# Expert pieces on pairs of token tiles with bf16 turns, and the pieces beside the score units gathered in a new order

## The chip, the cores and the metric

The kernel runs on one core of one Trainium2 chip. Times are device microseconds (us) of that core, over many executions. For one core an execution more than 1.5% above the fastest of the same kernel counts as slow. The limit for "faster" or "slower" is 2%.

Engines: PE is the matrix engine, PEld its weight loads, DVE the vector engine, ACT the scalar (activation) engine, POOL GpSimd, SP the engine that issues most DMA transfers. PSUM is the memory in which the tiles that PE writes are kept here (the kernel's pools psc and psm among them). The granted clock is the share of its full speed that the chip allowed PE, as the profile records it.

## The reference

```python
# clustered attention: a query sees only keys of its own cluster
q_assign = argmax(q_n @ c_n.T); k_assign = argmax(k_n @ c_n.T)      # 16 clusters per head
mask = q_assign[:, :, :, None] == k_assign[:, :, None, :]
scores = where(mask, q @ k.T / 8, -1e9)                              # B 4, H 8, S 768, D 64
x = (softmax(scores) @ v) laid out as [3072 tokens, 512]
# mixture of adapters: two of eight experts of rank 16 for each token
w = softmax of the two largest of x @ w_gate
out = x + sum over both of w * ((x @ A[e]) @ B[e])
```

## The kernel before

Work goes by pairs of heads, 16 of them, and a pair has three steps of 256 queries. In each step PE makes six score units (sc, two matmuls each; ACT takes the exponential into ET; DVE and POOL add up ET for the softmax sums, sp and sm) and twelve value products (od, seen as 24 matmuls in the trace). Four pairs make one batch, 768 tokens; the experts of a batch run during the next four pairs. The small pieces go into the gaps between the score units: each step has slots 0 to 5 (behind score unit 0 to 5), "pre" (ahead of the value products) and "post" (behind them).

The small pieces, by the name of the tile that PE writes: tp (turns of q and k), rt (cluster scores) and its turn rn, from which DVE makes mx and the one-hot rows oh; oT (oh turned), copied to os_ and sent by DMA into the score operands augA and augB; dp (softmax sums over partitions) and its turn dn; xp (turn of the output, scaled into xn); lp and lt (gate logits). "Turn" means a transpose on PE. All of them share three PSUM buffers.

```python
def prep_onehot(p):                       # rn: needs rs, the DVE copy of rt
    rn_ps = psm.tile([128, HS], F32, name="rn_ps", tag="m")
    for i in range(3):
        nc.tensor.transpose(rn_ps[:, i * 128:(i + 1) * 128], s["rs"][:, i * 128:(i + 1) * 128], ident_f[:])
    ...                                   # mx, then oh, on DVE
def moe_x(b, ts, t):                      # one token tile, four fp32 turns
    xx = psm.tile([128, NDC, 128], F32, name="xx", tag="m")
    for dc in range(NDC):
        nc.tensor.transpose(xx[:, dc, :], xn_of[b][:, t, dc * 128:(dc + 1) * 128], ident_f[:])
    xTb = mo.tile([128, NDC, 128], BF16, name="xTb")
    nc.scalar.copy(xTb[:], xx[:])
# moe_z: four matmuls, DVE copy z_s; moe_g: the gate, twelve small operations, mostly DVE;
# moe_t: zg on DVE, turn zT_ps, DVE copy zT
def moe_l(b, ts, t):
    dl = psm.tile([128, DX], F32, name="dl", tag="m")
    nc.tensor.matmul(dl[:], ms.pop((b, "t", t))[:], b_b[:])
    ot = mo.tile([128, DX], F32, name="ot", bufs=4)
    nc.vector.tensor_tensor(ot[:], dl[:], xn_of[b][:, t, :], ALU.add)
    nc.sync.dma_start(out_b[:, t, :], ot[:])          # 256 KB
...
        for n in range(NS - 1):
            for i in range(6):
                scores(*divmod(n + 1, NT), i)
                run(n, i)                 # the pieces of slot i
            run(n, "pre")
            for kc in range(T):
                pv(n // NT, n % NT * T + kc)
            run(n, "post")
        p = NP - 1                        # the end
        den_sum(p)
        while mq:                         # expert pieces that are left
            moe()
        den_turn(p)
        normalize(p, 0)
        normalize(p, 1)
        logit_tiles(p, [0, 1, 2, 3])
        queue_moe(B - 1, [0, 1, 2, 3])
        moe(3)
        for kc in range(T):
            pv(p, 2 * T + kc)             # the last value products
        moe(3)
        normalize(p, 2)
        logit_tiles(p, [4, 5])
        queue_moe(B - 1, [4, 5])
        while mq:
            moe()
```

The softmax here doesn't subtract the row's maximum and nothing guards it: scores larger than these inputs give would overflow.

## Time and profile before

377.38 us, median of 6 executions (376.52 to 379.69). The profiled one spans 377.7 us. The page's busy times, and the chain of waits that ended last, followed back from the last instruction, with shares of the span:

```profile
PE 346.8 (92%) x2866; PEld 242.1 (64%) x2872; DVE 275.9 (73%) x479; ACT 243.6 (65%) x449; POOL 187.4 (50%) x157
...
PE 75%; DVE 12%; DMA 5%; ACT 3%; issue 3%; SPq 1%; DVEq 0%; ACTq 0%
```

PE is nearly always busy and makes up three quarters of the chain, so a shorter PE stream should shorten the kernel. The PE timeline of a step shows how its score units are broken up. Columns: start, length, engine, line, operation, tiles, shapes, count, and in brackets an idle stretch with what ended it:

```profile
89.29 0.50 PE L244 MATMUL sc<-augA 80*128 80x256 f32 x2
89.63 0.40 PE L244 MATMUL sc<-augB 80*128 80x256 f32 x2
89.86 0.49 PE L295 MATMUL dn<-ident_f,ds 128*128 128x128 f32 x3
90.11 0.48 PE L244 MATMUL sc<-augA 80*128 80x256 f32 x2
90.50 0.55 PE L203 MATMUL rn_ps<-ident_f,rs 128*128 128x128 f32 x3
90.81 0.48 PE L244 MATMUL sc<-augB 80*128 80x256 f32 x2
91.13 0.38 PE L308 MATMUL xp<-ident_f,OT 128*128 128x128 f32 x2
...
101.87 0.47 PE L244 MATMUL sc<-augA 80*128 80x256 f32 x2 [0.48 <-ACT OT L274]
```

Lengths overlap (89.29 + 0.50 reaches past 89.63), so the distance from start to start is what a group costs. A unit that follows a unit takes about 0.235 us (89.63 to 89.86), one that follows another piece about 0.32 (90.81 to 91.13). The 0.48 us at 101.87 is laid to ACT's OT, which had been done for long; the program's own waits at that instruction include the DMA that brings the one-hot rows. Three stretches will be compared below. They are cut at the start of the third step's value products of pair 4 and of pair 14 (pairs are counted from 0): 124.87 us to the first cut, 212.87 us for pairs 5 to 14, and 39.97 us for the rest, "the end". Plain pairs, without expert work, repeat every 19.5 us, the others take 20.2 to 22.5.

### The profile page before, as it was taken

How to read it: one execution, taken by the hardware profiler on the slowest of the kernel's cores; microseconds unless marked ns; L12 is line 12 of the kernel's file. 1: busy time of each engine (PE TensorE's matmuls, PEld its weight loads, DVE VectorE, ACT ScalarE, POOL GpSimd, SP SyncE). 2: the span in 40 equal slices, each digit the busy share in tenths (PEclk: the TensorE clock that was granted, in tenths of full speed). 3: DMA queues.
4: the chain of work that ended last, by engine and by line, in shares of the span. 5: the costliest groups of instructions: out<-in, count | busy, mean ns of one | idle time of the engine just before them, and what ended most of it. 6: DMA issues, size and time to landing. Idle time of an engine off the chain costs nothing.

```text
span 377.7 us, 7587 instructions
## 1 busy us (share of the span) xinstructions
PE 346.8 (92%) x2866; PEld 242.1 (64%) x2872; DVE 275.9 (73%) x479; ACT 243.6 (65%) x449; POOL 187.4 (50%) x157
## 2 busy tenths in 40 slices
PE   8798699999999999999999999999999999999773
PEld 3475567676767766675767766675666777667441
DVE  3463275969689876788699875789689876788765
ACT  3374557677686877675686876675686877666321
POOL 1057154756556455457356455547457455556300
PEclk9959699999999999999999999999999999999998
DMA  9367652616171706146281705137271302020204
GB/s 168 69 166 149 137 126 44 146 32 160 22 168 21 169 12 130 50 103 170 78 196 22 169 8 128 55 90 183 76 197 25 83 7 45 14 77 28 86 9 159
DMA packets 66340, 35.66 MB, mean 94 GB/s; under 512 B 56960, under 2 KB 61056, under 8 KB 66304
## 3 DMA queue, kind: packets, MB, share of 16 engines
q1 hardware_dynamic: 64592, 34.76, 38.7%
q10 hardware_dynamic: 1712, 0.43, 0.6%
q8 instruction: 22, 0.36, 0.4%
q14 instruction: 14, 0.11, 0.1%
HBM read 19.45 MB, written 6.29 MB: 68 GB/s over the span
## 4 chain that ended last, share of the span: by engine, by line
PE 75%; DVE 12%; DMA 5%; ACT 3%; issue 3%; SPq 1%; DVEq 0%; ACTq 0%
PE od L269 30%; PE sc L244 18%; PE tp L172 4%; PE dp L282 3%; PE rt L191 3%; DVE sp L248 3%; PE lp L323 2%; PE xx L370 2%; PE warm_ps L100 2%; PE oT L220 2%; PE rn_ps L203 2%; ACT ET L245 2%; PE xp L308 2%; PE dn L295 2%; DMA augB<-augA 2%
## 5 line engine op out<-in xcount | busy, mean ns | idle before, releaser
L245 ACT ACTIVATE ET<-sc,expbias 128x512 f32<-128x512 f32 x288 | 180.3, 698 | 19.2 <-PE sc L244 17.8
L248 POOL TENSOR_TENSOR sp<-ET 128x512 f32<-128x512 f32 x48 | 71.3, 1486 | 153.9 <-ACT ET L245 153.9
L269 PE MATMUL od<-ET,v_nat 128*64 128x256 f32 x1152 | 137.3, 388 | 1.4 <-DVE zT L430 1.2
L269 PEld LDWEIGHTS od<-ET,v_nat 128*64 128x64 f32 x1152 | 79.5, 139 | 48.4 <-issue 11.5
L250 POOL TENSOR_TENSOR sp<-sp,ET 128x512 f32<-128x512 f32 x48 | 74.8, 1559 | 7.1 <-ACT ET L245 4.3
L244 PE MATMUL sc<-augA 80*128 80x256 f32 x288 | 70.5, 327 | 8.1 <-DMA augA<-os__424 3.4
L244 PE MATMUL sc<-augB 80*128 80x256 f32 x288 | 69.9, 325 | 0.2 <-DMA augB<-os__249 0.2
L244 PEld LDWEIGHTS sc<-augA 80*128 80x128 f32 x288 | 45.6, 196 | 31.7 <-issue 24.3
L274 ACT COPY OT<-od 128x256 f32<-128x256 f32 x48 | 17.8, 371 | 72.7 <-PE od L269 72.7
L250 DVE TENSOR_TENSOR sp<-sp,ET 128x512 f32<-128x512 f32 x48 | 59.3, 1235 | 3.8 <-ACT ET L245 3.0
L248 DVE TENSOR_TENSOR sp<-ET 128x512 f32<-128x512 f32 x48 | 33.4, 697 | 35.5 <-ACT ET L245 35.5
L251 DVE TENSOR_TENSOR sm<-sp 128x256 f32<-128x256 f32 x48 | 58.1, 1211 | 0.8
L244 PEld LDWEIGHTS sc<-augB 80*128 80x128 f32 x288 | 45.5, 197 | 2.8 <-ACT ET L245 0.8
L251 POOL TENSOR_TENSOR sm<-sp 128x256 f32<-128x256 f32 x48 | 38.2, 796 | 3.6
L312 DVE TENSOR_TENSOR xn<-xp,rr 128x256 f32<-128x256 f32 x48 | 19.9, 416 | 3.0 <-PE xp L308 2.8
L437 DVE TENSOR_TENSOR ot<-dl,xn 128x512 f32<-128x512 f32 x24 | 16.2, 682 | 7.2 <-PE dl L435 7.2
L308 PE MATMUL xp<-ident_f,OT 128*128 128x128 f32 x96 | 18.2, 272 | 0.0
L172 PE MATMUL tp<-ident_f,q_nat 128*128 128x128 f32 x96 | 16.0, 277 | 1.7 <-DMA q_nat<-in_q_dram 1.5
L374 ACT CAST xTb<-xx 128x512 bf16<-128x512 f32 x24 | 14.2, 599 | 5.0 <-PE xx L370 4.9
L172 PE MATMUL tp<-ident_f,k_nat 128*128 128x128 f32 x96 | 16.3, 282 | 0.0
L282 PE MATMUL dp<-sm,ones_138 128*32 128x384 f32 x128 | 14.2, 498 | 1.0 <-DVE sm L251 1.0
L340 DVE TENSOR_TENSOR lgp<-lt,rr 128x96 f32<-128x96 f32 x15 | 3.9, 258 | 15.1 <-PE lt L336 15.1
(187 smaller groups left out, 347.5 us busy)
## 6 DMA issues: line engine op xcount, KB each, us to landing
q_nat<-in_q_dram SPq DMA_DIRECT2D x32, 192.0 KB, 3.7
augB<-augA SPq DMA_DIRECT2D x16, 384.0 KB, 4.6
v_nat<-in_v_dram SPq DMA_DIRECT2D x16, 384.0 KB, 4.3
out_dram<-ot SPq DMA_DIRECT2D x24, 256.0 KB, 2.3
k_nat<-in_k_dram SPq DMA_DIRECT2D x30, 192.0 KB, 4.1
k_nat<-in_k_dram ACTq DMA_DIRECT2D x2, 192.0 KB, 4.7
b_f<-in_moe_B_dram SPq DMA_DIRECT2D x1, 256.0 KB, 4.4
a_f<-in_moe_A_dram SPq DMA_DIRECT2D x4, 64.0 KB, 3.0
```

The lines of the kernel that those rows point to most:

```text
L172: nc.tensor.transpose(tp[:, i * 128:(i + 1) * 128], src[:, t, :, :].rearrange("p a d -> p (a d)"), ident_f[:],)
L244: nc.tensor.matmul(sc[:, i, :], au[0:80, k0:k0 + 128], au[0:80, cs])
L245: nc.scalar.activation(ET[:, 2 * kp:2 * kp + 2, :], sc[:], ACTF.Exp, bias=expbias[:], scale=SCALE)
L248: eng.tensor_tensor(sp[:], ET[:, 0:2, :], ET[:, 2:4, :], ALU.add)
L250: eng.tensor_tensor(sp[:], sp[:], ET[:, 4:6, :], ALU.add)
L251: eng.tensor_tensor(s["sm"][a][:, cs], sp[:, 0, :], sp[:, 1, :], ALU.add)
L269: nc.tensor.matmul(s["od"][64 * a:64 * a + 64], s["v"][:, a, kc, :], s["ET", th][a][:, kc, :], start=(kc == 0), stop=(kc == T - 1), tile_p ...
L274: nc.scalar.copy(s["OT"][:, cs], s["od"])
L282: nc.tensor.matmul(dp[r:r + 32, :].rearrange("p (n i) -> p n i", i=128), ones32[:], s["sm"][a][:].rearrange("p (n h i) -> p h n i", h=2, i ...
L308: nc.tensor.transpose(xp[:, i, :, :].rearrange("p a d -> p (a d)"), s["OT"][:, t * 128:(t + 1) * 128], ident_f[:],)
L312: nc.vector.tensor_tensor(xn_of[b][:, ts, j * 128:(j + 1) * 128].rearrange("p t (a d) -> p t a d", a=2), xp[:], s["rr"][:, ts].to_broadcas ...
L437: nc.vector.tensor_tensor(ot[:], dl[:], xn_of[b][:, t, :], ALU.add)
```

## The change

Its intent: fewer, longer groups on PE (a unit behind a switch costs 0.32 us, not 0.235), with the one-hot pieces early enough to hide their DMA, and expert turns in bf16 on two token tiles at a time, so that half as many pieces and copies are needed. The core of the diff:

```diff
+PLAN = (   # piece, (step of the pair, slot); 6 is "pre", 7 is "post"
+    ("moe", (0, 1)), ("load_v", (0, 1)), ("t0", (1, 3)), ("moe", (1, 5)), ("moe", (1, 7)), ("t1", (2, 1)),
+    ("t2", (2, 1)), ("route", (2, 7)), ("load_qk", (2, 7)), ("den_sum", (2, 7)), ("onehot", (3, 1)),
+    ("den_turn", (3, 1)), ("norm0", (3, 4)), ("norm1", (3, 4)), ("mask", (3, 5)), ("logit_sum", (3, 7)),
+    ("logit_turn", (4, 3)), ("norm2", (4, 3)), ("queue", (4, 7)),
+)
-                put(n + 1, 4, prep_transpose, p + 2, 0)
-                put(n + 2, 0, prep_transpose, p + 2, 1)
-                put(n + 2, 2, prep_transpose, p + 2, 2)
-                put(n + 3, 2, prep_onehot, p + 2)
-                put(n + 4, 2, prep_mask, p + 2)
-                put(n + 3, 1, den_turn, p)
 ... (the other pieces likewise)
-            for i in ((0,), (3, 5), (3,))[n % NT]:
-                put(n, i, moe)
-    def moe_x(b, ts, t):
-        xx = psm.tile([128, NDC, 128], F32, name="xx", tag="m")
-            nc.tensor.transpose(xx[:, dc, :], xn_of[b][:, t, dc * 128:(dc + 1) * 128], ident_f[:])
+    def moe_x(b, ts, i):
+        xb = mo.tile([128, 2, DX], BF16, name="xb")
+        nc.vector.tensor_copy(xb[:], xn_of[b][:, t:t + 2, :])
+        xx = psm.tile([128, 2, NDC, 128], BF16, name="xx", tag="m")
+        for u in range(2):
+            for dc in range(NDC):
+                nc.tensor.transpose(xx[:, u, dc, :], xb[:, u, dc * 128:(dc + 1) * 128], ident_b[:])
 ... (moe_z, moe_t, moe_l likewise on two tiles; one store of 512 KB for two of 256 KB)
-        n = len(ts)
+        n = len(ts) // 2
```

More of the change, by code (lines that the diff above doesn't have):

```diff
@@ L69, with after @@
     st = {}
+    done = set()
+    def after(step, *needs):
+        assert all(x in done for x in needs), (step, needs)
+        done.add(step)
     def load_pair(p, which="qkv", keng=nc.sync):
@@ L163, in prep_transpose @@
     def prep_transpose(p, u):
+        after(("t", p, u), *[("t", p, i) for i in range(u)])
         s = st[p]
@@ L183, in prep_route @@
     def prep_route(p):
+        after(("route", p), ("t", p, 2))
         s = st[p]
@@ L199, in prep_onehot @@
     def prep_onehot(p):
+        after(("onehot", p), ("route", p))
         s = st[p]
@@ L216, in prep_mask @@
     def prep_mask(p):
+        after(("mask", p), ("onehot", p))
         s = st[p]
@@ L230, in scores @@
     def scores(p, th, ui):
+        after(("s", p, th, ui), ("mask", p))
         s = st[p]
@@ L274, in pv @@
             nc.scalar.copy(s["OT"][:, cs], s["od"])
+            after(("pv", p, th))
     def den_sum(p):
+        after(("den_sum", p), ("s", p, NT - 1, 5))
         s = st[p]
@@ L291, in den_turn @@
     def den_turn(p):
+        after(("den_turn", p), ("den_sum", p))
         s = st[p]
@@ L302, in normalize @@
     def normalize(p, th):
+        after(("norm", p, th), ("den_turn", p), ("pv", p, th))
         s = st[p]
@@ L317, in logit_sum @@
     def logit_sum(p):
+        after(("logit_sum", p), ("pv", p, NT - 1))
         s = st[p]
@@ L331, in logit_turn @@
     def logit_turn(p):
+        after(("logit_turn", p), ("logit_sum", p), ("den_turn", p))
         s = st[p]
@@ L365, with moe_z @@
     ms = {}
-    def moe_x(b, ts, t):
-        xx = psm.tile([128, NDC, 128], F32, name="xx", tag="m")
-        for dc in range(NDC):
-            nc.tensor.transpose(
-                xx[:, dc, :], xn_of[b][:, t, dc * 128:(dc + 1) * 128], ident_f[:],
-            )
-        xTb = mo.tile([128, NDC, 128], BF16, name="xTb")
+    def moe_x(b, ts, i):
+        t = ts[i]
+        xb = mo.tile([128, 2, DX], BF16, name="xb")
[4 more added lines that the diff above has]
+                nc.tensor.transpose(xx[:, u, dc, :], xb[:, u, dc * 128:(dc + 1) * 128], ident_b[:])
+        xTb = mo.tile([128, 2, NDC, 128], BF16, name="xTb")
         nc.scalar.copy(xTb[:], xx[:])
         ms[(b, t)] = xTb
-    def moe_z(b, ts, t):
+    def moe_z(b, ts, i):
         key = (b, "z", ts[0])
-        if t == ts[0]:
+        t = ts[i]
+        if i == 0:
             ms[key] = mo.tile([128, T, E * R], F32, name="z_s", bufs=1)
-        z = psm.tile([128, E * R], F32, name="z", tag="m")
+        z = psm.tile([128, 2, E * R], F32, name="z", tag="m")
         xTb = ms.pop((b, t))
-        for dc in range(NDC):
-            nc.tensor.matmul(z[:], xTb[:, dc, :], a_b[:, dc, :], start=(dc == 0), stop=(dc == NDC - 1))
-        nc.vector.tensor_copy(ms[key][:, t - ts[0], :], z[:])
+        for u in range(2):
+            for dc in range(NDC):
+                nc.tensor.matmul(z[:, u, :], xTb[:, u, dc, :], a_b[:, dc, :], start=(dc == 0), stop=(dc == NDC - 1))
+        nc.vector.tensor_copy(ms[key][:, i:i + 2, :], z[:])
     def moe_g(b, ts):
@@ L418, in moe_g, with moe_t, moe_l @@
         ms[(b, "g", ts[0])] = g
-    def moe_t(b, ts, t):
-        i = t - ts[0]
-        zg = mo.tile([128, E, R], BF16, name="zg")
+    def moe_t(b, ts, i):
+        zg = mo.tile([128, 2, E, R], BF16, name="zg")
         nc.vector.tensor_tensor(
-            zg[:], ms[(b, "z", ts[0])][:, i, :].rearrange("p (e r) -> p e r", e=E),
-            ms[(b, "g", ts[0])][:, i, :].unsqueeze(2).to_broadcast([128, E, R]), ALU.mult,
-        )
-        zT_ps = psm.tile([128, 128], BF16, name="zT_ps", tag="m")
-        nc.tensor.transpose(zT_ps[:], zg[:].rearrange("p e r -> p (e r)"), ident_b[:])
-        zT = mo.tile([128, 128], BF16, name="zT")
+            zg[:].rearrange("p u e r -> p (u e) r"),
+            ms[(b, "z", ts[0])][:, i:i + 2, :].rearrange("p u (e r) -> p (u e) r", e=E),
+            ms[(b, "g", ts[0])][:, i:i + 2, :].rearrange("p u e -> p (u e)").unsqueeze(2).to_broadcast([128, 2 * E, R]),
+            ALU.mult,
+        )
+        zT_ps = psm.tile([128, 2, 128], BF16, name="zT_ps", tag="m")
+        for u in range(2):
+            nc.tensor.transpose(zT_ps[:, u, :], zg[:, u].rearrange("p e r -> p (e r)"), ident_b[:])
+        zT = mo.tile([128, 2, 128], BF16, name="zT")
         nc.vector.tensor_copy(zT[:], zT_ps[:])
-        ms[(b, "t", t)] = zT
-    def moe_l(b, ts, t):
-        dl = psm.tile([128, DX], F32, name="dl", tag="m")
-        nc.tensor.matmul(dl[:], ms.pop((b, "t", t))[:], b_b[:])
-        ot = mo.tile([128, DX], F32, name="ot", bufs=4)
-        nc.vector.tensor_tensor(ot[:], dl[:], xn_of[b][:, t, :], ALU.add)
+        ms[(b, "t", ts[i])] = zT
+    def moe_l(b, ts, i):
+        zT = ms.pop((b, "t", ts[i]))
+        ot = mo.tile([128, 2, DX], F32, name="ot")
+        for u in range(2):
+            dl = psm.tile([128, DX], F32, name="dl", tag="m")
+            nc.tensor.matmul(dl[:], zT[:, u, :], b_b[:])
+            nc.vector.tensor_tensor(ot[:, u, :], dl[:], xn_of[b][:, ts[i] + u, :], ALU.add)
         out_b = out[b * S:(b + 1) * S, :].rearrange("(p t) d -> p t d", t=T)
-        nc.sync.dma_start(out_b[:, t, :], ot[:])
+        nc.sync.dma_start(out_b[:, ts[i]:ts[i] + 2, :], ot[:])
     mq = []
@@ L450, in queue_moe @@
     def queue_moe(b, ts):
-        n = len(ts)
+        if len(ts) == T:
+            for p in range(b * HP, (b + 1) * HP):
+                after(("moe", p), ("logit_turn", p), *[("norm", p, th) for th in range(NT)])
+        n = len(ts) // 2
         mq.append([("g", b, ts)])
@@ L454, in queue_moe @@
             for i in range(n + 1):
-                piece = [(first, b, ts, ts[i])] if i < n else []
+                piece = [(first, b, ts, 2 * i)] if i < n else []
                 if i > 0:
-                    piece.append((second, b, ts, ts[i - 1]))
+                    piece.append((second, b, ts, 2 * (i - 1)))
                 mq.append(piece)
@@ L481 @@
     with tc.manual_schedule(engines={PE}):
-        plans = [{} for _ in range(NP * NT + 4)]
+        plans = [{} for _ in range(NP * NT + 8)]
         def put(n, i, *call):
@@ L487 @@
         for p in range(NP):
-            n = NT * p
-            if p + 2 < NP:
-                put(n, 1, load_pair, p + 2, "v")
-                put(n + 1, 4, prep_transpose, p + 2, 0)
-                put(n + 2, 0, prep_transpose, p + 2, 1)
-                put(n + 2, 2, prep_transpose, p + 2, 2)
-                put(n + 3, 2, prep_onehot, p + 2)
-                put(n + 4, 2, prep_mask, p + 2)
-            if p < NP - 1:
-                put(n + 2, "post", den_sum, p)
-                if p + 2 < NP:
-                    put(n + 2, "post", prep_route, p + 2)
-                    put(n + 2, "post", load_pair, p + 3, "qk")
-                put(n + 3, 1, den_turn, p)
-                put(n + 3, 3, normalize, p, 0)
-                put(n + 3, 4, normalize, p, 1)
-                put(n + 3, "pre", logit_sum, p)
-                put(n + 4, 0, logit_turn, p)
-                put(n + 4, 1, normalize, p, 2)
-                if p % HP == HP - 1:
-                    put(n + 4, 1, queue_moe, p // HP, list(range(T)))
+            calls = {"load_v": (load_pair, p + 2, "v"), "load_qk": (load_pair, p + 3, "qk"),
+                     "t0": (prep_transpose, p + 2, 0), "t1": (prep_transpose, p + 2, 1),
+                     "t2": (prep_transpose, p + 2, 2), "route": (prep_route, p + 2),
+                     "onehot": (prep_onehot, p + 2), "mask": (prep_mask, p + 2),
+                     "den_sum": (den_sum, p), "den_turn": (den_turn, p),
+                     "norm0": (normalize, p, 0), "norm1": (normalize, p, 1), "norm2": (normalize, p, 2),
+                     "logit_sum": (logit_sum, p), "logit_turn": (logit_turn, p),
+                     "queue": (queue_moe, p // HP, list(range(T)))}
+            for name, (step, slot) in PLAN:
+                if name in ("den_sum", "den_turn", "norm0", "norm1", "norm2", "logit_sum", "logit_turn"):
+                    ok = p < NP - 1
+                elif name == "queue":
+                    ok = p < NP - 1 and p % HP == HP - 1
+                elif name == "load_qk":
+                    ok = p + 3 < NP
+                elif name == "moe":
+                    ok = True
+                else:
+                    ok = p + 2 < NP
+                if ok:
+                    put(NT * p + step, slot, *calls.get(name, (moe,)))
         put(0, 1, prep_onehot, 1)
@@ L511 @@
         NS = NP * NT
-        for n in range(NS):
-            for i in ((0,), (3, 5), (3,))[n % NT]:
-                put(n, i, moe)
         def run(n, i):
@@ L523 @@
                 run(n, i)
-            run(n, "pre")
+            run(n, 6)
             for kc in range(T):
                 pv(n // NT, n % NT * T + kc)
-            run(n, "post")
+            run(n, 7)
         p = NP - 1
```

## The prediction

> **What bounds it now.** PE is 92% busy (busy table) and holds 75% of the chain of waits; DVE holds 12%. After the prologue (about 45 us) each pair of heads is three steps: score units and small pieces, then a 2.74 us value product (od), and once per pair dp and rt, 1.43 us. Starts in the PE timeline: plain pairs repeat every 19.5 us (65.6, 85.1, 104.6); pairs with expert work take 20.2 to 22.5, about 7 us more per batch of four. Idle PE gaps (groups, waits) are small: 0.5 us per plain pair where the first score unit waits for the one-hot rows' DMA into augA (shown as waiting for ACT OT), and 0.65 to 0.75 us per expert pair where lp waits for DVE's oh. ACT (65%) and DVE (73%) are busy but looser.
>
> **What a group switch costs.** From start-to-start times on PE: a score unit after another takes 0.235 us, one after a different piece 0.32. A pair has 18.
>
> **What the change removes.**
> 1. Fewer groups: the plain pair goes from about 13 broken runs of units to 7. Sum over a pair: about 5.9 to 5.1 us.
> 2. The mask pieces come a whole step earlier, so the 0.5 us DMA wait goes.
> 3. Expert turns: six groups of four fp32 transposes (0.44 us each) per batch become three of eight bf16 ones (estimate 0.5 to 0.55 each, from oT at 75 ns and z at 50 to 60 ns per matmul): 1 us per batch. [...] Half as many expert pieces and fewer waits for zT: 0.7 us per batch.
>
> **What it adds.** Twelve casts of 128x1024 to bf16 on DVE. [...] the augA cast shows it (1536 columns in 0.953 us against 512 columns of sp in 0.697). Estimate 0.65 us each; most are hoisted into slack. Pairing z, zg, zT copies returns about half of that.
>
> **What gives part back.** The one-hot turns (rn) now come two units after dp, but need rs, which waits on DVE behind the previous step's sp and sm (1.3 + 1.3 us), which wait for the fifth exponential on ACT. Worked through with trace durations, rs lands about 2.8 us after od ends, while PE reaches rn at 2.0: a new wait of 0.7 to 1.0 us per pair. The second xp waits about 0.2 us for oh. So the plain pair comes to about 18.8 to 19.0 us, not the 17.9 of PE work alone: the loop exponential, sums, rs, rn, oh is nearly as long as PE's.
>
> **Sum.** 15 pairs x 0.6 = 9 us; experts 4 x 1.7 = 6 us less about 1 us at the end (one 512 KB store last instead of 256 KB). Predicted 364.0 us, range 354 to 373. Faster by over 2%: 0.74; within 2%: 0.24; slower: 0.02.
>
> **What would show it.** Right: plain pairs at 18.5 to 19.1 us; no score unit waiting for augA's one-hot DMA; score units mostly 0.235; rn waiting for DVE rs 0.5 us or more; xx groups at 0.5 to 0.6 us; DVE busy a few us higher; xb about 0.65 us. Wrong: rn not waiting and plain pairs at 18 us (then 355 or less).
>
> **What would make it wrong.** Bursts of four units with four PSUM buffers could stall on ACT; in expert steps DVE has 7 us in line before rs, so rn could wait 2 us; xb at 1 us or more if POOL contends; or rs comes earlier than reckoned, and the full gain appears.

What the profile of the kernel before shows is times alone: a load of 128x128 bf16 weights (z) took 98 ns, one of fp32 weights (tp, xp, xx) 140 to 145; the augA cast took 0.953 us for 1536 columns, which by proportion is 0.64 us for 1024, about the 0.65 estimated for a cast xb. The sum: as written it comes to 9 + 6 - 1 = 14 us (4 x 1.7 is 6.8, written as 6).

## The result

375.98 us median (372.07 to 380.46, 20 executions) against 378.05 for the kernel before in the same rounds (40 executions). The ratio of fast runs is 0.9901, 95% interval 0.9872 to 0.9931: a gain of 1%. A ratio here is the mean time of one kernel's fast runs over that of the other's of the same rounds, so it is not quite the ratio of the medians quoted. The prediction was 364.0 with a range of 354 to 373: wrong. The profiled run was 374.2 us long. Its busy times and chain:

```profile
PE 341.3 (91%) x2870; PEld 242.9 (65%) x2872; DVE 281.6 (75%) x455; ACT 243.2 (65%) x437; POOL 181.8 (49%) x157
...
PE 53%; DVE 25%; ACT 9%; issue 4%; DMA 4%; POOL 1%; SPq 1%; DVEq 0%; ACTq 0%; POOLq 0%
```

PE lost only 5.5 us of busy time, and its share of the chain fell from 75% to 53%: DVE and ACT have come into the chain. The same part of a plain pair as shown of before:

```profile
104.15 0.50 PE L260 MATMUL sc<-augA 80*128 80x256 f32 x2
104.49 0.39 PE L260 MATMUL sc<-augB 80*128 80x256 f32 x2
105.48 0.55 PE L217 MATMUL rn_ps<-ident_f,rs 128*128 128x128 f32 x3 [0.60 <-DVE rs L209]
105.86 0.49 PE L314 MATMUL dn<-ident_f,ds 128*128 128x128 f32 x3
106.11 0.48 PE L260 MATMUL sc<-augA 80*128 80x256 f32 x2
106.43 0.40 PE L260 MATMUL sc<-augB 80*128 80x256 f32 x2
106.67 0.40 PE L260 MATMUL sc<-augA 80*128 80x256 f32 x2
```

The units now run together at 0.24 us, and rn waits 0.60 us for rs, the DVE copy that stands behind the sums. A plain pair takes 18.99 us. Up to here the prediction holds. PE's waits, sorted by total (us in total, times, longest):

```profile
PE rn_ps L217 <- DVE rs L209: 9.2, 11, 2.1
...
PE xx L396 <- DVE xb L392: 2.1, 1, 2.1
PE dp L300 <- DVE sm L267: 2.0, 1, 2.0
PE zT_ps L456 <- DVE zg L448: 1.9, 2, 1.0
```

Three of these waits reached about 2 us. What followed one of them, at the first expert pair:

```profile
125.92 0.72 PE L217 MATMUL rn_ps<-ident_f,rs 128*128 128x128 f32 x3 [2.06 <-DVE rs L209]
126.44 0.85 PE L314 MATMUL dn<-ident_f,ds 128*128 128x128 f32 x3
127.08 1.06 PE L396 MATMUL xx<-ident_b,xb 128*128 128x128 bf16 x8
127.90 0.78 PE L260 MATMUL sc<-augA 80*128 80x256 f32 x2
```

The score unit at 127.90 takes 0.57 us to the next one, not 0.32. The reason is in the table of windows of the same profile (stretch, its length, then busy time and count of PE, PEld, DVE, ACT and POOL, then the granted PE clock, the DMA share and GB/s):

```profile
123.00:126.00 3.00, 0.94 (x9) 0.61 (x6) 2.83 (x3) 1.67 (x3) 2.04 (x2) 1.00 0.94 237
126.00:129.50 3.50, 3.50 (x21) 3.44 (x22) 1.90 (x4) 1.32 (x2) 0.00 (x0) 0.52 0.12 27
...
345.00:348.00 3.00, 0.86 (x9) 0.20 (x9) 1.31 (x2) 0.48 (x1) 1.05 (x1) 1.00 0.43 175
348.00:351.50 3.50, 3.12 (x21) 2.31 (x22) 1.95 (x6) 0.27 (x1) 0.00 (x0) 0.50 0.00 0
351.50:355.00 3.50, 3.43 (x28) 2.41 (x27) 2.76 (x11) 2.24 (x3) 0.00 (x0) 0.52 0.00 0
...
362.00:365.00 3.00, 0.62 (x8) 0.45 (x8) 2.77 (x11) 0.74 (x2) 0.00 (x0) 1.00 0.70 288
365.00:368.50 3.50, 1.56 (x11) 1.03 (x12) 1.65 (x6) 0.52 (x1) 0.00 (x0) 0.51 0.02 5
```

After each of these three stretches, in which PE worked less than a third of the time, the granted clock is halved for a while, although after the first two PE is busy (3.50 of 3.50 us, and 3.12 + 3.43 of 7.00; behind the third 1.56 of 3.50). The halved stretches of all profiles are 3.4, 6.8 or 10.2 us long, except where the program's end cuts one. What gives the clock back is not shown: in the prologue of the change PE was busy throughout from 20.35 to 30.59 us, and the clock stayed halved all that time. Which waits a halved clock follows is worked out in the last section.

Where the time went, by the three stretches defined above (us; from the profiles, so one execution each):

| kernel | to pair 4 | pairs 5 to 14 | the end | span |
|---|---|---|---|---|
| before | 124.87 | 212.87 | 39.97 | 377.7 |
| the change, predicted (sums of the terms) | 121.9 | 202.6 | 38.7 | 363.2 |
| the change | 118.96 | 209.64 | 45.58 | 374.2 |

For the predicted row, each of 16 pairs is given its 0.6 us, 2.5 batches of 1.7 us lie in the middle, and the end has one pair, one batch and the 1 us of loss. That allotment is mine; it adds up to 14.5 us, where the prediction wrote 9 + 6 - 1. The first stretch did better than predicted, but 2.2 us of the 5.9 that it gained lie ahead of the third step of pair 0 (45.7 against 43.5 us), and there the profiles of the change and its variants spread from 42.2 to 44.6 anyway. The middle is 7.0 us short and the end 6.9 us: it takes 5.6 us more than before, where 1.3 us less was predicted.

### The profile page after: what moved, and what is told of

It reads as the page before. It is cut to its first block, busy times and chain, and to the rows that moved or that the text cites. A ratio compares the mean times of both kernels' runs of the same rounds, so it can differ in the third digit from the quotient of the medians.

```text
span 374.2 us, 7520 instructions
## 1 busy us (share of the span) xinstructions
PE 341.3 (91%) x2870; PEld 242.9 (65%) x2872; DVE 281.6 (75%) x455; ACT 243.2 (65%) x437; POOL 181.8 (49%) x157
## 4 chain that ended last, share of the span: by engine, by line
PE 53%; DVE 25%; ACT 9%; issue 4%; DMA 4%; POOL 1%; SPq 1%; DVEq 0%; ACTq 0%; POOLq 0%
PE od L285 20%; PE sc L260 13%; ACT ET L261 6%; DVE sp L266 6%; DVE sm L267 5%; DVE sp L264 3%; PE tp L184 3%; PE xp L328 2%; PE rn_ps L217 2%; PE warm_ps L111 2%; PE lp L344 2%; PE z L410 2%; DVE xb L392 2%; PE xx L396 2%; DMA v_nat<-in_v_dram 2%
## 5 line engine op out<-in xcount | busy, mean ns | idle before, releaser
L264 POOL TENSOR_TENSOR sp<-ET 128x512 f32<-128x512 f32 x48 | 67.3, 1403 | 150.1 <-ACT ET L261 150.1
L285 PEld LDWEIGHTS od<-ET,v_nat 128*64 128x64 f32 x1152 | 87.5, 139 | 34.6 <-issue 4.0
L260 PE MATMUL sc<-augB 80*128 80x256 f32 x288 | 61.3, 295 | 0.4 <-DMA augB<-os__249 0.2
L266 DVE TENSOR_TENSOR sp<-sp,ET 128x512 f32<-128x512 f32 x48 | 56.0, 1166 | 7.4 <-ACT ET L261 6.6
L267 DVE TENSOR_TENSOR sm<-sp 128x256 f32<-128x256 f32 x48 | 51.6, 1076 | 1.1
L264 DVE TENSOR_TENSOR sp<-ET 128x512 f32<-128x512 f32 x48 | 39.6, 825 | 10.2 <-ACT ET L261 10.0
L260 PEld LDWEIGHTS sc<-augB 80*128 80x128 f32 x288 | 45.7, 196 | 2.0 <-ACT ET L261 1.5
L332 DVE TENSOR_TENSOR xn<-xp,rr 128x256 f32<-128x256 f32 x48 | 19.6, 419 | 1.9 <-PE xp L328 1.2
L306 ACT COPY ds<-dp 128x384 f32<-128x384 f32 x16 | 7.7, 479 | 18.6 <-PE dp L300 18.6
L217 PE MATMUL rn_ps<-ident_f,rs 128*128 128x128 f32 x48 | 9.1, 301 | 9.3 <-DVE rs L209 9.2
L222 DVE TENSOR_REDUCE mx<-rn_ps 128x24 f32<-128x384 f32 x16 | 8.9, 558 | 11.2 <-PE rn_ps L217 11.2
L398 ACT COPY xTb<-xx 128x1024 bf16<-128x1024 bf16 x12 | 12.3, 1024 | 7.6 <-PE xx L396 7.5
```

Source lines behind the costliest of these rows:

```text
L260: nc.tensor.matmul(sc[:, i, :], au[0:80, k0:k0 + 128], au[0:80, cs])
L264: eng.tensor_tensor(sp[:], ET[:, 0:2, :], ET[:, 2:4, :], ALU.add)
L266: eng.tensor_tensor(sp[:], sp[:], ET[:, 4:6, :], ALU.add)
L267: eng.tensor_tensor(s["sm"][a][:, cs], sp[:, 0, :], sp[:, 1, :], ALU.add)
L285: nc.tensor.matmul(s["od"][64 * a:64 * a + 64], s["v"][:, a, kc, :], s["ET", th][a][:, kc, :], start=(kc == 0), stop=(kc == T - 1), tile_p ...
L332: nc.vector.tensor_tensor(xn_of[b][:, ts, j * 128:(j + 1) * 128].rearrange("p t (a d) -> p t a d", a=2), xp[:], s["rr"][:, ts].to_broadcas ...
```

## The experiments

Theory A: what is gained before is lost to new waits of PE on DVE (rn on rs in most pairs, and at the end), and the longest of these also halve the clock. The rivals are named at the runs. Every run was correct. Each ratio is against the kernel before in the same rounds; the change itself stands at 0.9901 (0.9872 to 0.9931). Against the kernel before, only e9 and e10 are "faster" by the 2% rule; e1, e2, e6 and e11 are "same", and e3, e4, e5, e7, e8 and e12 "unclear", their intervals reaching over 0.98. The intervals of e6 and e11 overlap that of the change. One execution of the kernel before in the rounds of e9 to e12 took 1489.89 us; it counts as slow and is left out.

| run | median us | ratio, 95% interval | to pair 4 | pairs 5 to 14 | the end |
|---|---|---|---|---|---|
| e1 order only | 379.02 | 0.9983, 0.9940 to 1.0026 | 118.22 | 213.65 | 42.57 |
| e2 experts only | 380.60 | 1.0037, 0.9999 to 1.0074 | 126.31 | 211.76 | 42.00 |
| e3 turns later | 370.68 | 0.9796, 0.9750 to 0.9843 | 117.65 | 204.83 | 45.44 |
| e4 end kept busy | 371.83 | 0.9805, 0.9769 to 0.9841 | 118.98 | 206.87 | 42.85 |
| e5 last piece later | 371.22 | 0.9815, 0.9779 to 0.9852 | 119.56 | 206.94 | 42.92 |
| e6 last cast early | 375.07 | 0.9898, 0.9854 to 0.9941 | slow profile | | |
| e7 = e3 + e5 + e6 | 370.84 | 0.9810, 0.9766 to 0.9855 | 119.94 | 204.31 | 44.67 |
| e8 cast on POOL | 369.57 | 0.9774, 0.9737 to 0.9810 | 118.04 | 205.21 | 44.05 |
| e9 = e3 + e5 + e8 | 362.90 | 0.9565, 0.9525 to 0.9605 | 118.34 | 202.19 | 41.42 |
| e10 = e9, end kept busy | 363.56 | 0.9581, 0.9538 to 0.9623 | 118.18 | 201.63 | 42.09 |
| e11 rn kept busy | 373.82 | 0.9866, 0.9825 to 0.9907 | 119.89 | 208.19 | 45.40 |
| e12 last two singly | 374.12 | 0.9753, 0.9685 to 0.9822 | 119.25 | 208.80 | 41.83 |

### e1 and e2: each half alone

e1 is the change with the expert functions of before and their four slots; e2 is the kernel before with the expert functions of the change.

```diff
 e1  -    ("moe", (0, 1)), ..., ("moe", (1, 5)), ("moe", (1, 7)), ...
     +    ("moe", (0, 0)), ..., ("moe", (1, 3)), ("moe", (1, 5)), ..., ("moe", (2, 3)), ...
     (moe_x, moe_z, moe_t, moe_l and the queue as before)
 e2  (moe_x, moe_z, moe_t, moe_l and the queue as in the change, nothing else)
```

> The new order with the expert part of before (single tiles, fp32 turns, four slots per pair). Theory A (the plain pair is held at 19.0 us by the loop of exponential, sums, rs, rn, and what is gained until 329 us is lost in the last 45 us to PE waits of 2 us, after which the clock is halved): plain pairs at 19.0 us, rn still waits about 0.6 us in each; expert pairs gain only about 0.5 us each against before; leftover expert pieces shorten the wait of dp at the end, so the end loses less than in the change: total about 371 to 375. Rival B (the paired expert pieces with their casts on DVE eat the gain, the order alone would give all that was hoped for): 366 or less.

> The order of before with the paired bf16 expert part. Theory A: the stretch up to the last two steps gains about 1 us per batch (PE work 5.5 to 4.5 us per batch), the end loses about 2 to 4 us against before because the last tiles now go as one pair and PE waits over 1 us for xb and xTb; total within 2 us of before (375 to 379). Rival B: the stretch with expert pieces is slower than before by 1 us or more per batch, total 380 or more.

Neither half gains alone. e1 has the plain pairs at 18.99 us with the same 0.6 us wait of rn, but its middle is 0.8 us longer than before, not a little shorter; its time, 379.02, missed both expectations, theory A's 371 to 375 as well as the rival's. e2 gained 1.1 us in the middle, less than expected, and lost 2.0 us at the end, as expected, and 1.4 us ahead of pair 4; its 380.60 is above the 375 to 379 of theory A. It meets the 380 or more of rival B, but not for the reason given, a slower middle. So rival B in its simple form (the order alone would give all) falls. The halves do not add: -0.8 and +1.1 us in the middle alone, and 3.2 together (5.9 in e5, which has the same middle without a halved clock). That the new slots and the fewer pieces were made for each other fits this, but no run isolates it.

### e3: rn one unit later

```diff
-    ("onehot", (3, 1)), ... ("mask", (3, 5)),
+    ("onehot", (3, 2)), ... ("mask", (3, 7)),
```

> The change with rn one score unit later, and the mask pieces behind the value product instead of ahead of it. Theory A: rn waits 0.3 us less for rs, oT no longer waits for oh, so a plain pair falls from 19.0 to 18.5 to 18.8, and the 2.06 us stall at the first expert pair shrinks below 1.7 us; total 3 to 8 us below the change (366 to 371). Rival C (the loop does not bind, the wait only moves to another place): plain pairs stay at 19.0 within 0.1, total as the change.

370.68 us, ratio 0.9796. A plain pair takes 18.43 us and rn no longer waits, which PE's timeline of this run shows:

```profile
83.60 0.39 PE L260 MATMUL sc<-augB 80*128 80x256 f32 x2
83.99 0.55 PE L314 MATMUL dn<-ident_f,ds 128*128 128x128 f32 x3
84.29 0.49 PE L260 MATMUL sc<-augA 80*128 80x256 f32 x2
84.61 0.52 PE L217 MATMUL rn_ps<-ident_f,rs 128*128 128x128 f32 x3
```

Moving rn behind dn and one more score unit removes the wait for the price of one switch. (The same edit moves the mask pieces from slot 5 to behind the value products; the two were not tried apart.) Rival C (the wait only moves) falls for the plain pairs. In the expert pairs there is a new one, though: once per batch tp waits 1.28 us for os_, since the scheduler put two casts xb ahead of os_ on DVE.

### e4: dummies in the waits of the end

Matmuls on constant data into a free score buffer, read by nobody, ahead of dp (9), dn (3), lpt (2), the first zT of the four tiles (3; the text says the second) and the last xx (9), z (5) and zT (5). They take no wait away; they keep PE busy in it.

> The change with matmuls that nobody reads put where PE waits at the end: ahead of dp, dn, lpt, the second zT and the last xx, z and zT. They take no wait away. Theory A: the granted clock stays at 1.00 to the end, where it fell to 0.5 in two stretches of 4 to 6 us; the last 33 us shrink by 2 to 4 us, total 371 to 373 and the runs at 376 to 380 become fewer. Rival D (the lower clock costs nothing since only waits count there, or it has another cause): no gain, or a loss of up to 2 us.

By the change's clock records the two stretches were 6.8 us long (from 348.0) and 9.1 (from 365.1 to the end), not 4 to 6.

371.83 us, 0.9805. In the profile the clock stays full from 43 us until 1.1 us before the end, and the end falls from 45.58 to 42.85 us, although every dependency is as it was. The largest part lies ahead of the last value products, which start 24.0 us after the third step's value products of pair 14 instead of 25.5. So, by these two profiles, 2.7 us of what the end lost are the halved clock. Rival D falls for this kernel. The profile of e12 (below) shows the same without dummies: dp waits as long there, the clock happens to stay full behind it, and the last value products start 24.0 us after that cut too.

```profile
345.92 0.85 PE L300 MATMUL dp<-sm,ones 128*32 128x384 f32 x8 [2.00 <-DVE sm L267]
```

### e5: the last expert piece behind the sums

```diff
-                    ok = True
+                    ok = (p, step, slot) != (NP - 1, 1, 5)
```

The last piece of the third batch (two dl on PE, two ot on DVE) stood ahead of the last value products of the loop. On DVE, in the change:

```profile
341.56 0.69 DVE L467 TENSOR_TENSOR ot<-dl,xn 128x512 f32<-128x512 f32 x1 [0.57 <-PE sc L260]
342.16 1.64 DVE L264 TENSOR_TENSOR sp<-ET 128x512 f32<-128x512 f32 x1
343.73 0.68 DVE L467 TENSOR_TENSOR ot<-dl,xn 128x512 f32<-128x512 f32 x1
344.33 1.16 DVE L266 TENSOR_TENSOR sp<-sp,ET 128x512 f32<-128x512 f32 x1
345.52 0.83 DVE L267 TENSOR_TENSOR sm<-sp 128x256 f32<-128x256 f32 x1
```

> The change, with the last expert piece of the third batch (two dl, two ot) put behind the last value product of the loop instead of ahead of it, so that its two ot (1.36 us on DVE) stand behind the last sums and its dl fill the wait of dp. Theory A: dp's wait falls from 2.0 us to under 1.0, the clock no longer halves at 348 to 355 us, and the time from the last od of pair 14 to the end falls from 58.0 us by 3 to 4.5: total 371.5 to 373. Rival F (dp waits for the last exponentials on ACT, the ot only happen to be there): the wait stays above 1.7 us, total as the change.

371.22 us, 0.9815; the six executions lie between 370.8 and 371.5. In e5, PE at the same place:

```profile
342.09 0.38 PE L466 MATMUL dl<-b_b,zT 128*128 128x512 bf16 x1 [0.16 <-issue]
343.25 1.34 PE L300 MATMUL dp<-sm,ones 128*32 128x384 f32 x8 [0.78 <-DVE sm L267]
```

The wait of dp fell from 2.02 to 0.78 us, the clock stayed full until 361 us, and the end took 42.92 us. Rival F falls. The kernel before had two ot there too, and dp waited 0.97 us: its first ot began 0.66 us ahead of those value products (0.11 in the change), and the sum behind it took 0.68 us, not 1.64.

### e6 and e7: the last cast early

e6 puts the turns of the last two token tiles, and with them their cast, ahead of the last logits. e7 joins e3, e5 and e6.

```diff
         normalize(p, 2)
+        moe_x(B - 1, [4, 5], 0)
         logit_tiles(p, [4, 5])
-        queue_moe(B - 1, [4, 5])
         while mq:
             moe()
+        for f in (moe_g, moe_z, moe_t, moe_l):
+            f(B - 1, [4, 5], *([] if f is moe_g else [0]))
```

> The change, with the cast of the last two token tiles ahead of the adds of the two before them on DVE, and their turns ahead of the last logits on PE. Theory A: the last xx no longer waits 2.06 us for xb, the clock does not halve at 365 us, the end from the last od on falls from 32.5 us by 2 to 3: total 372.5 to 374. Rival G (the gate's chain of small DVE operations ends the program anyway, as before the change, where zT waited 1.9 us for zg): the wait moves to zT, gain under 1 us.

> The later turns of the third run together with the two changes of the end. Theory A: the gains add, since they lie in different stretches: 5 + 3.5 + 2.5 us off the change, 362 to 366. If they do not add (above 368), one of the waits is behind another.

e6: 375.07 us, 0.9898, no gain over the change. Its profile fell in a slow execution, so only the order of its waits is read from it: xx still waited 1.78 us for the cast, and zT 2.98 us for zg, which needs the gate, which needs the logits that now came later. As rival G wrote, the wait moves to zT and the gain stays under 1 us. But e6 itself delays the logits, so it does not show that the gate's chain would end the program with the logits in their old place, and e12 (2.2 us where rival G expected under 0.7) does not fit it; this stays open. e7 missed its 362 to 366: 370.84 us, no better than e3 alone. Its end takes 44.67 us where e5's takes 42.92, with the same 2.98 us wait of zT.

### e8: the cast on POOL

```diff
-        nc.vector.tensor_copy(xb[:], xn_of[b][:, t:t + 2, :])
+        nc.gpsimd.tensor_copy(xb[:], xn_of[b][:, t:t + 2, :])
```

> The change, with the cast of the token tiles on POOL instead of DVE (9.6 us of DVE work moved to the engine that is 49% busy). Rival B (the casts on DVE are what hold rs and so PE back in the expert pairs): the first expert pair falls from 21.6 or more to under 21.0 us, total 371 to 374. Theory A: the casts were mostly in slack; POOL takes longer for them and its sums come later, xx waits for xb at the end longer than 2 us; total 375 to 380.

369.57 us, 0.9774: better than either side had written down. A cast takes 1.18 us on POOL against a mean of 0.82 on DVE, but POOL has room (it is busy 49% of the change's span). The first expert pair stays at 21.63 us, so the casts are not what makes that pair long. They cost elsewhere: the pair in which a batch is queued took 19.6 to 20.0 us in e5 and takes 18.97 to 18.99 here, and the end takes 44.05 us instead of 45.58, with the same 2.02 us wait of dp and the same halved clock after it. The pair behind the queueing one did not grow for it: the two take 40.6 us together, against 41.2 to 41.5 in e5. My statement that the casts lie in slack was wrong, for about 0.8 us per batch and 1.5 at the end.

### e9 and e10: the version that beats both

e9 = e3 + e5 + e8. e10 adds dummies at the end as in e4 (four ahead of dp).

> Three edits that each gained alone, together: turns one unit later, the last expert piece behind the last value product, the cast on POOL. Theory A: plain pairs 18.4 us, expert pairs under 21, no stall on t0 behind the casts, dp's wait under 1 us; from the change as it ran here they should take 5 + 3 + 3 us: 363 to 366. If one of them only moved a wait that another makes as well, 367 or more.

> The same with unread matmuls in the remaining PE waits at the end. Theory A (the halved clock costs time of its own): 1 to 2 us below the run without them, 362 to 364. Rival D: no difference within 0.5 us.

e9: 362.90 us (361.43 to 363.84), 0.9565, which is 4.35% below the kernel before and just better than expected. The first expert pair of a batch missed its "under 21": 20.87 to 21.24 us. Its busy times and chain:

```profile
PE 338.5 (94%) x2870; PEld 235.1 (65%) x2872; DVE 276.1 (76%) x443; ACT 243.1 (67%) x437; POOL 196.5 (54%) x169
...
PE 71%; DVE 14%; DMA 5%; ACT 5%; SPq 2%; issue 2%; POOL 0%; DVEq 0%; ACTq 0%
```

PE is the chain again. The middle stretch, 202.19 us, is what the prediction had reckoned for the change (202.6), and the total is near its 364.0; but it took three further edits, so this is no support for the prediction. e3 and e5 together without the cast on POOL were not run. e10 shows the limit of the clock argument: dummies kept the clock at 0.981 in its profile against 0.964, and both spans are 361.9 us (the medians differ by 0.66 us, to the loss of e10, with overlapping intervals). Behind the prologue, the clock of e9 is halved only in the last 9 us, where PE mostly waits for DVE, ACT and POOL. There rival D is right: no gain.

### e11: dummies in rn's wait

```diff
+        if p > 1:
+            for wi in range(3):
+                nc.tensor.matmul(rn_ps[:], wdummy[:, 0:128], wdummy[:, 0:HS], start=(wi == 0), stop=(wi == 2))
```

> The change with three unread matmuls (0.5 us) written into rn's own buffer ahead of rn in each pair, inside its wait for rs, and nothing else. They shorten the stretch in which PE stands still without taking the wait away. Theory A (the slower executions of the change, 375 to 380 us, are those in which a wait of 2 us at the first expert pair of a batch halves the clock for 3.4 us or more): the plain pairs stay at 19.0 us, no halved clock between 50 and 340 us in the profile, and all runs lie at 371 to 374. Rival (the spread of the runs has another source, as in the end): the runs spread from 372 to 379 as before. The dummies themselves may cost up to 0.1 us per pair.

373.82 us, six executions from 373.35 to 375.61, where the change spread from 372.07 to 380.46. The profile has no halved clock between 44 and 348 us, and this is its first expert pair:

```profile
124.64 0.66 PE L218 MATMUL rn_ps<-wdummy 128*128 128x384 bf16 x3
126.64 0.55 PE L220 MATMUL rn_ps<-ident_f,rs 128*128 128x128 f32 x3 [1.34 <-DVE rs L209]
127.03 0.49 PE L317 MATMUL dn<-ident_f,ds 128*128 128x128 f32 x3
127.35 0.61 PE L399 MATMUL xx<-ident_b,xb 128*128 128x128 bf16 x8
```

rn comes nearly as late as in the change's profile (6.75 us after the cut ahead of this pair, against 6.96; 0.5 us of dummies and 1.34 us of idle), but the pieces behind it run at full clock, xx in 0.61 us and not 1.06. The pair takes 22.53 us where the change's took 24.34. Two of the six executions, 375.27 (the profiled one) and 375.61, missed the expected 371 to 374. Theory A's account of the slow pair holds. That it makes all of the spread is not shown: e5 had no spread either, without dummies there.

### e12: the last two token tiles singly

The functions of before, for tiles 4 and 5 of the last batch only (fp32 turns, one tile each, stores of 256 KB).

> The change with the last two token tiles taken singly and turned in fp32 as before. Theory A: at the end the pair of tiles is a longer serial chain (cast, eight turns, one copy of 1.0 us, eight z, one store of 512 KB) than two tiles that overlap: the end shrinks by 1.5 to 2.5 us, total 373 to 374.5. Rival G (the gate's chain ends the program): under 0.7 us.

Inconclusive as a time: three of its six executions were slow, and the 0.9753 rests on the three fast ones. From the profile (a fast one): from the start of the last value products to the end 17.85 us, against 20.06 in the change and 18.49 before. That is 2.2 us, within what theory A expected, but the two halve the clock at different places, so not all of it is the length of the chain. By chance this profile also shows the slow expert pair again, 24.35 us with a wait of 2.07 us, in the second batch instead of the first.

## Why the prediction was wrong

- "PE is 92% busy ... and holds 75% of the chain": right, and the gain from grouping is real. The score units run at 0.238 us (median of 75 between units) as reckoned.
- "the 0.5 us DMA wait goes": right, no such wait is left in the loop's plain pairs.
- "a new wait of 0.7 to 1.0 us per pair", "the plain pair comes to about 18.8 to 19.0 us": right, 0.60 us and 18.99 us. e3 showed that this wait is real and avoidable: 18.43.
- xx "0.5 to 0.55" us for eight bf16 turns: 0.42 to 0.46 from start to start. A weight load fell from 140 to 110 ns. This term was even a little better.
- xb "0.65 us each; most are hoisted into slack": the size was right when undisturbed (0.68 us), but 3 of 12, each begun while a POOL sum sm ran, took 1.22 us, and "into slack" failed. e8 got about 0.8 us per batch and 1.5 us at the end by moving them to POOL.
- "experts 4 x 1.7 = 6 us": failed. Here lies about half of the shortfall of 7.0 us in the middle. In e5, whose middle had no halved clock, pairs 5 to 14 gained 5.9 us; with 0.5 us per pair from the plain part, an estimate, 0.9 us is left for the experts, where 4.25 was predicted. e2, the experts alone, gained 1.1. The waits of rn, reckoned at one size for all pairs, are 0.6 to 1.0 us in most expert pairs and 2.06 in one, since DVE has the gate, z_s, zg, zT and ot in the same queue. The prediction named this as a risk ("rn could wait 2 us") but gave it no term.
- The halved clock was not in the prediction at all. In the profiled run the middle is 2.7 us longer than in e5 (209.64 against 206.94), the later rs included. Of that 0.8 us is no loss: pair 4, ahead of the cut, was as much shorter (18.99 against 19.79). Pairs 4 and 5 together take 43.3 us, against 41.5 in e5 and 41.5 in e11, where rn is late too but the clock stays full. So the halved clock cost about 1.8 us there.
- "less about 1 us at the end (one 512 KB store last ...)": the term that failed most. The end got 5.6 us longer. The store was harmless (2.6 us to landing against 2.3). What it missed: two ot of 0.68 us stand among the last sums, later than before, so dp waited 2.02 us (e5 took 1.2 of it away); that wait halved the clock (e4: 2.7 us); and the last pair of tiles is a serial chain behind DVE (e12, up to 2.2 us). These overlap and are not to be added.

Next, why rn waits 0.97 us in some executions of the same code and 2.06 in others. In the change's profile DVE's first sum ahead of that rn took 1.77 us, in e4's only 0.68. DVE in the change:

```profile
120.22 0.95 DVE L191 CAST augA<-qk_1398 128x1536 fp32r<-128x1536 f32 x1
121.08 1.77 DVE L264 TENSOR_TENSOR sp<-ET 128x512 f32<-128x512 f32 x1
122.95 1.58 DVE L266 TENSOR_TENSOR sp<-sp,ET 128x512 f32<-128x512 f32 x1
```

and in e4:

```profile
119.66 0.95 DVE L198 CAST augA<-qk 128x1536 fp32r<-128x1536 f32 x1
120.53 0.68 DVE L271 TENSOR_TENSOR sp<-ET 128x512 f32<-128x512 f32 x1
121.32 1.58 DVE L273 TENSOR_TENSOR sp<-sp,ET 128x512 f32<-128x512 f32 x1
```

In the change a POOL add had begun 0.53 us earlier and ran until 122.30 us; in e4 POOL's add began 0.18 us after DVE's. POOL in the change, then in e4:

```profile
120.55 1.75 POOL L264 TENSOR_TENSOR sp<-ET 128x512 f32<-128x512 f32 x1 [2.20 <-ACT ET L261]
...
120.71 1.65 POOL L271 TENSOR_TENSOR sp<-ET 128x512 f32<-128x512 f32 x1 [3.39 <-ACT ET L268]
```

So the length of the DVE add goes with what POOL does at its start. The change's own trace has eight first sums begun during a POOL instruction: seven ended 0.547 to 0.551 us behind its end, one took 0.67. By a count over all 14 profiles, they hold 672 such first sums on DVE. The 598 at whose start no POOL instruction ran took 0.66 to 0.69 us. Of the 66 that began with over 0.2 us of a POOL instruction still to run, 62 ended 0.54 to 0.55 us behind its end; the other four took 0.67 to 0.68. So in these profiles a DVE add that begins behind POOL's nearly always ends behind it; by what mechanism is not shown. In the change this add was 1.09 us longer than in e4, and rn waited 1.09 us longer; the add also began 0.57 us later after the cut, and sm gave as much back (0.83 us, in e4 1.39). Still open is why the order differs from one execution to the next.

## What to carry to other kernels

PE was 92% busy here, and shortening its stream paid only until the next loop of dependencies was as long (a plain pair fell from 19.5 to 18.99 us, with 0.60 us of it a new wait; 18.43 without that wait); ask which copy the regrouped piece waits for, and put one independent piece between. DVE, which did both the kernel's sums and the side work's adds one after another, set PE's waits here (dp waited 2.02 us with two ot among the last sums, 0.78 without them): look at what stands in front of the instruction that PE needs, above all at the end of the program, where nothing fills a wait. A PE wait of 2.02 to 2.07 us could cost twice here, once as a wait and once as half a clock for the 3.4 us or more behind it, where PE was what the time hung on.

## When the clock was halved, what that cost, and what a switch cost

- Waits of 2.02 to 2.07 us were enough to halve it (the change at 125.9, 346.5 and 363.9 us, e12 at 208.1), although PE had worked 0.94 of the 3.0 us ahead of the first halving. Yet the wait of 2.00 us of dp in e12 halved nothing. In the profiles of the kernel before and of the change, all clock changes lie whole multiples of 3.413 us apart (in the change 44.24 to 126.16 us is 24 of them), and the shortest halved stretch is one. An estimate with stretches of that measured length, laid back from e12's next halving at 358.8 us, puts a bound at 345.1 us, inside that wait (343.9 to 345.9). Laid so over the profiles of before and change, each from its own clock changes, the stretches sort themselves: of 201 at full clock, the eight in which PE was busy (by the profile, which models the ends of matmuls) for 0.21 to 0.41 of the time were all followed by a halved one, the 193 with 0.64 or more never. A count over all 14 profiles has 1333 at full clock: the 31 with up to 0.54 were all followed by a halved one, the 1299 above 0.56 never, and two of the three between. In the change the three waits left shares of 0.21 to 0.40; in e12 the wait of dp was split over two stretches, 0.65 and 0.58. So in these profiles the busy share of such a stretch tells what followed, and the length of one gap does not; how the chip decides is not shown.
- The halved clock cost nothing at the end of e9: it is halved there for 9.1 us, in e10 for 0.5, and the end is not longer for it (41.42 us against 42.09); the spans are both 361.9 us.
- Switching PE between groups of matmuls of different operands: a score unit took about 0.235 us behind another and 0.32 behind a different piece.
